# RetNet attention and maxout FFN on one core: blocks 6 and 7 worked in chunks

## The chip, the cores and the metric

One core of a Trainium2 chip runs the whole kernel. The metric is device time in microseconds of one execution. Besides the runs that give the time there is one profiled execution, from which all rows come.

## The reference

```python
# q, k, v: (8, 8, 576, 64) float32
scores = scale * q @ k.T
gamma = 1.0 - 2.0 ** (-5.0 - arange(8))                # one per head
Dmat = where(rel >= 0, gamma ** rel, 0.0)              # rel = row - column
attn = (scores * Dmat) @ v
x = attn.transpose(0, 2, 1, 3).reshape(4608, 512)
h = maximum(maximum(x @ w1, x @ w2), x @ w3)           # w: 512 x 768, float64 in memory
out = h @ w_out                                        # 768 x 512
```

The decay is a geometric one, so the kernel works in blocks of rows and carries a state (a sum of k times v) from block to block within a sequence.

## The kernel before, in words

The 4608 rows are cut into 36 blocks `g` of 128 rows. Four blocks make a tile `t` of 512 rows for the FFN; there are nine tiles. While `ffn(t)` runs the products of tile t, the list `steps(t + 1)` puts the attention steps of the next four blocks between them: the last loop of the kernel goes through twelve slots `at(0)` to `at(11)`, runs the steps of a slot, and then takes the next piece of `ffn(t)`. Each engine executes its instructions in the order in which they were recorded; semaphores hold an instruction until its inputs and its buffer are there. Nothing is scheduled at run time. Loads are issued on SP, the queue engine; a load that waits for its buffer holds all later loads.

For each block there are these steps:

- `load` brings k, q and v in rows (`kraw`, `qraw`, `vraw`). For blocks from `BY_PE` on, q is not brought in rows: `load_blocks` (L223) brings q and a second copy of k (`kxraw`) in squares of 32 by 32. Each of its DMAs moves 32 KB.
- `transposes` (L275): for blocks below `BY_PE`, TensorE transposes k and q in 128 by 128 tiles (L295, results `kt`, `qt`) and ScalarE copies them out (L296). From `BY_PE` on, VectorE does a StreamTranspose of 32 by 32 squares, one instruction for k and one for q, and the layout of the load does the rest.
- `decay` multiplies v by a factor; for blocks from `CPT + 2` = 6 on it is a list `scaling` of eight small ScalarE multiplies (L209), one for each head, that are put between other work, or all at once by `scores`.
- `scores`: the products k times q, and k times v for the state. Blocks 0 to 3 are in one form; below `BY_CHUNKS` is `parity_scores` (L322, L327, masks L338, states L346 and L348); from `BY_CHUNKS` on is `chunk_scores` (L377, L380; mask L384, states L392 on VectorE and a multiply L394 on GpSimd). Both use 64 matmuls of 64 by 64 for a pair of blocks away from the ends of a sequence.
- `values`: the products of the masked scores with v (L505 or L527), and of the old state with q (L496 or L534), for two blocks at once. `parity_values` makes the second in two halves, with two small ScalarE copies between them, which read what the first half wrote:

```python
        old(0)
        for m in range(2):
            nc.scalar.copy(first[:], o[m][:, 0, 0, 0:1])

        def rest():
            old(1)
            between.append(partial(chunk_output, o, chunks, t, i))

        between.append(rest)
```

- `chunk_output` then writes the result, scaled, into `xT`, the FFN's input; the last pair of a tile also starts the sums `xS`. What lies in `between` is recorded at the next place where `ffn` takes it.
- `carry` copies the parity form's state into the chunk form's state once, at the first block by chunks; `state_factors` copies the factors `gs_of`.

Tile 0 of the FFN is special. It is done in plain products: `up` (L930, nine units of two 128 x 512 results each), with maxima on VectorE (L935), then `down` (L917). In this time the weights arrive as float64 and are converted by ScalarE and VectorE (`convert`). A unit of the table `middles` has attention steps after its first result. From tile 1 on (first product at 119.04 us) the FFN is done in fewer products of sums (L905), which need the weight sums that VectorE makes at the end of tile 0. So blocks 4 to 7 are worked within tile 0, under `steps(1)`, with a, b, c, d = 4, 5, 6, 7.

Buffers that matter: q in rows or squares has two buffers `q` (blocks 2 and 5 have one of their own), `kx` has two, k three and one more; four PSUM banks `r` serve scores, values and, from block 4 on, TensorE's transposes.

Of the kernel before, what the change touches and what calls it, by code (L numbers as in the profile page):

```python
# [49 lines left out]
C = 128  # L50
NT = 4 * C
NH = NT // 2
BY_PE = 8
BY_CHUNKS = 8
AHEAD = 3
FILL = 160
PARTS = 11
# [42 lines left out]
def kernel(  # L100
# [14 lines left out]
    nc = tc.nc  # L115
    P = 128
# [3 lines left out]
    NP = H // 2  # L120
# [1 line left out]
    NDC = DM // P  # L122
    NF = DF // P
    CPT = NT // C
    assert B * S % C == 0 and S % D == 0 and BY_CHUNKS % CPT == 0 and S >= C and N % NT == 0 and NT % P == 0 and 2 * D == P and NP == NDC

    const = ctx.enter_context(tc.tile_pool(name="const", bufs=1))
    raw = ctx.enter_context(tc.tile_pool(name="raw", bufs=AHEAD + 1))
# [17 lines left out]
    def half(j):  # L146
        return slice(D * j, D * (j + 1))
# [59 lines left out]
    def scale(n=1):  # L207
        for _ in range(min(n, len(scaling))):
            scaling.popleft()()  # L209
# [33 lines left out]
                        src[b, :, pos:pos + 32, 32 * a:32 * a + 32].rearrange("h p i -> p h i"))  # L243

    def load(g, names="kqv"):
        if g >= BY_PE and ("q", g) not in raws:
            load_blocks(g, *range(C // 32))
        for n, src in (("k", k), ("q", q), ("v", v)) if g < BY_PE else (("k", k), ("v", v)):
            if n not in names:
                continue  # L250
            bufs = {"k": 3, "q": 2, "v": 4}[n]
            pool, bufs = (raw0, 1) if n != "v" and g < BY_PE and g % (bufs + 1) == bufs else (raw, bufs)
            if n == "v":
                t = vpool.tile([C, H, D], FP32, tag="v", name="vraw")
            else:
                t = pool.tile([C, H, D], FP32, tag=n, name=n + "raw", bufs=bufs)
            raws[n, g] = t
            for row, b, pos, m in spans(g):
                nc.sync.dma_start(t[row:row + m], src[b, :, pos:pos + m, :].rearrange("h p d -> p h d"))
# [147 lines left out]
        for j in range(2):  # L407
            nc.scalar.copy(stacked(g)[half(0), j::2, :], states[g][half(j)])

    def state_factors():  # L410
        for j in range(2):
            nc.scalar.copy(gs_of[half(0), j::2], gs[half(j)])

# [106 lines left out]
    def chunk_values(chunks, t, i):  # L520
        o = [ps_r.tile([P, 2, NP, D], FP32, tag="r", name="o") for _ in range(2)]
        cross = ((0, 0), (1, 1), (0, 1), (1, 0))
        for n, g in enumerate(chunks):
            for u in range(NP):
                for m, c in cross:
                    h = head(c, u)
                    nc.tensor.matmul(o[m][half(c), n, u, :], lhsT=vds[g][half(m), h, :], rhs=sts[g][half(m), h, :],  # L527
                                     start=n == 0 and u == 0, stop=place(g, m) == 0, skip_group_check=True)
        for n, g in enumerate(chunks):
            for u in range(NP):  # L530
                for m, c in cross:
                    h = head(c, u)
                    if place(g, m) > 0:
                        nc.tensor.matmul(o[m][half(c), n, u, :], lhsT=stacks[g][half(m), h, :],  # L534
                                         rhs=qks[g]["q"][half(m), h, :], start=False, stop=True, skip_group_check=True)
        chunk_output(o, chunks, t, i)

    def chunk_output(o, chunks, t, i):
        if i == 0:
# [420 lines left out]
    def ffn(t):  # L960

        h = hpool.tile([P, NF, NT], FP32, tag="h", name="h")
        if t == 0:
            a, b, c, d = range(CPT, 2 * CPT)
            middles = {units[2]: [(transposes, a)], units[3]: [(scores, a)], units[5]: [(scores, b)],
                       units[8]: [(scores, c, d)]}
            for fp, i in units:
                if (fp, i) == units[0]:
                    first_ups(h)
                    yield  # L970
                    continue
                for fb in (2 * fp, 2 * fp + 1):
                    maximum, = up_plain(t, h, fb, i)
                    if (fp, i) == units[-1] and fb % 2:
                        maximum()
                        convert(2)
                    else:
                        convert(4 if (fp, i) == units[1] else 2)
                        maximum()
                    for step, *blocks in middles.get((fp, i), ()) if fb == 2 * fp else ():  # L980
                        for g in blocks:
                            step(g)
                    scale(3)
                    if between:
                        between.pop()()
                yield
            convert(3)
            for fb, _ in enumerate(downs_plain(t, h, range(NF // 2))):
                convert(4 * len(pieces) if fb else 2)
                scale(4)  # L990
                if fb == 1:
                    while_converting.close()
                    late["pool"] = ctx.enter_context(tc.tile_pool(name="late", bufs=1))
                    state_factors()
                    nc.gpsimd.tensor_copy(causal[half(1), 0:D], causal[half(1), half(1)])
                    late_room()
                    weight_sums(0)
                if fb == 2:
                    between.pop()()
                chore((0, 2, 6, 6, len(chores), 0)[fb])  # L1000
                if fb == 3:
                    between.pop()()
                if fb in (1, 3):
                    yield
            yield
            return
        order = (0, 2, 1)
        if t == 1:
            spread.append(True)
            weight_sums(2)  # L1010
            weight_sums(1)
            form_groups = seven_forms(order)
        if t == 2:
            out_sums(order)
        total = len(order) * 2 * len(PRODUCTS)
        count = parts = 0
        for fp in order:
            while fp not in summed_fp:
                chore()
            for step, _ in enumerate(up(t, h, fp)):  # L1020
                if step % 4 == 1 or step % 4 == 3 and len(urgent) > (2 if t == 1 else 6):
                    chore(len(urgent) > 0)
                elif chores:
                    chores.popleft()()
                if step % 3 == 2:
                    scale()
                if t == 1 and fp == order[-1] and step == 19:
                    chores.extend(form_groups[0])
                count += 1
                if count * (NF // 2 * 3) >= (parts + 1) * total:  # L1030
                    parts += 1
                    yield
            if t == 1:
                seven_hidden(h, fp)
            elif fp != order[-1]:
                chores.extend(sums_of_hidden(h, order, 3 - order.index(fp)))
        chore(len(urgent) + len(chores))
        if t == 1:
            for n, _ in enumerate(downs_seven(t, order)):
                if n == 0:  # L1040
                    for step in form_groups[1]:
                        step()
                chore(4)
                scale(2)
                if n in (1, 3):
                    yield
        else:
            for n, _ in enumerate(downs(t, h, order)):
                chore(2)
                scale()  # L1050
                if n in (3, 9):
                    yield
        yield
# [52 lines left out]
    def steps(t):  # L1106
# [12 lines left out]
        if t == 1:  # L1119
            a, b, c, d = range(CPT, 2 * CPT)  # L1120
            at(0, (load, a, "kq"))
            at(1, (load, a, "v"))
            at(2, (load_weights, 2), (load, b, "kq"))
            at(3, (decay, a), (load, b, "v"), (load, c, "kq"))
            at(4, (transposes, b), (load, c, "v"))
            at(5, (decay, b), (load, d))
            at(6, (decay, c), (load_blocks, d + 1, 0))
            at(7, (values, [a, b]), (transposes, c), (finish_values, b), (decay, d), (convert, 2),
               (load_blocks, d + 1, 1, 2))
            at(8, (transposes, d), (load_blocks, d + 1, 3), (load, d + 1))  # L1130
            at(9, (load_blocks, d + 2, 0, 1))
            at(10, (values, [c, d]), (decay, d + 1), (load_blocks, d + 2, 2))
            at(11, (load_blocks, d + 2, 3), (load, d + 2), (transposes, d + 1))
            return todo
        for n in range(0, CPT, 2):
            a, b, m = CPT * t + n, CPT * t + n + 1, 6 * (n // 2)
            first_pair = a == BY_CHUNKS
            s = m + 2 if first_pair else m + 1
            at(m - (n > 0), (transposes, b))
            if first_pair:  # L1140
                at(m, (decay, b), (load, a + 2), (carry, a))
            at(s, (scores, a), (scores, b), (load, b + 2))
            at(s + 1, (decay, a + 2))
            at(s + 2, (decay, b + 2))
# [60 lines left out]
```

## Time and profile before

| | |
|---|---|
| median of 3 runs | 740.6 us (740.52 to 742.5) |
| profiled execution, its own time | 740.45 us |
| its span | 738.7 us |
| TensorE / VectorE / ScalarE / GpSimd busy | 733.8 / 568.8 / 356.6 / 36.4 us |
| granted TensorE clock | 1.0 |
| DMA | 58.85 MB, mean 80 GB/s; 222 to 261 GB/s in the first 74 us |

The span is what the trace sees from the first to the last instruction; the time has 1.75 us more around it. A row of the timeline gives start and length in us, engine, line, operation, output from input, sizes and the number of records; in brackets stands the idle time of the engine before it and what ended it. A matmul of float32 shows as two records. Lines of the kernel are written L295. A wait row gives who waited for whom: total, times, the longest.

### The profile page before, as it was taken

Reading aid. Unit: us, or ns where it says so; the run is one execution under the profiler, and the core shown is the slowest. Engines: PE = TensorE matmul, PEld = TensorE weight load, DVE = VectorE, ACT = ScalarE, POOL = GpSimd, SP = SyncE. Lnnn points to the kernel's source line nnn. Section 1 sums busy time; section 2 is a strip of 40 time slices with the busy share of each in tenths; the row PEclk is TensorE's granted clock in tenths of the full one; section 3 lists DMA queues with packets and bytes.
Section 4 is the critical chain, followed back from the end, with each engine's and each line's share of the span. In section 5 each row is a group of like instructions: output and inputs, shape, how many; then the busy total and the mean of one; then the engine's idle time right before and its main releaser. Section 6 shows DMA issues by size and latency. Waiting matters only on the chain.

```text
span 738.7 us, 17318 instructions
## 1 busy us (share of the span) xinstructions
PE 733.8 (99%) x6948; PEld 606.1 (82%) x6948; DVE 568.8 (77%) x1051; ACT 356.6 (48%) x746; POOL 36.4 (5%) x42
## 2 busy tenths in 40 slices
PE   9999999999999999999999999999999999999998
PEld 7654546888888888888888888888888888888887
DVE  5998697999886895699658876787768966893676
ACT  4896934554245534544354525543455255424441
POOL 2000000122000100010000000000100010000000
PEclk9999999999999999999999999999999999999999
DMA  9999523414251515141524243332514150000001
GB/s 222 243 246 261 120 54 85 87 24 93 68 97 29 96 37 104 40 87 39 109 50 75 48 107 60 60 58 58 115 23 94 42 121 14 1 31 29 0 1 57
DMA packets 226640, 58.85 MB, mean 80 GB/s; under 512 B 207872, under 2 KB 225280, under 8 KB 226560
## 3 DMA queue, kind: packets, MB, share of 16 engines
q1 hardware_dynamic: 225584, 57.71, 36.0%
q8 instruction: 54, 0.88, 0.5%
q14 instruction: 26, 0.21, 0.1%
q10 hardware_dynamic: 976, 0.04, 0.1%
HBM read 48.27 MB, written 9.44 MB: 78 GB/s over the span
## 4 chain that ended last, share of the span: by engine, by line
PE 99%; DVE 0%; ACT 0%; issue 0%
PE a L905 20%; PE b L905 17%; PE c L905 9%; PE up L930 9%; PE di L751 7%; PE d L905 6%; PE e L905 6%; PE dhc L751 5%; PE deg L751 3%; PE sk L377 3%; PE down L917 3%; PE o L527 2%; PE dfd L751 2%; PE o L534 2%; PE dx L658 1%; PE kv L380 1%
## 5 line engine op out<-in xcount | busy, mean ns | idle before, releaser
L893 DVE TENSOR_TENSOR part<-part 128x512 f32<-128x512 f32 x168 | 117.8, 701 | 86.4 <-ACT part L890 83.8
L890 ACT COPY part<-b 128x512 f32<-128x512 f32 x120 | 70.3, 586 | 163.6 <-PE b L905 161.0
L893 DVE TENSOR_TENSOR h<-h,part 128x512 f32<-128x512 f32 x120 | 83.2, 693 | 24.9 <-ACT h L890 20.5
L890 ACT COPY part<-a 128x512 f32<-128x512 f32 x96 | 56.3, 586 | 51.6 <-PE a L905 51.1
L209 ACT ACTIVATE vraw<-vraw,gk 128x64 f32<-128x64 f32 x240 | 76.8, 347 | 0.1
L905 PE MATMUL b<-s,n 128*128 128x256 f32 x288 | 73.9, 379 | 0.0
L930 PE MATMUL up<-xT,w 128*128 128x512 f32 (+2 forms) x160 | 64.0, 554 | 0.0
L905 PEld LDWEIGHTS b<-s,n 128*128 128x128 f32 x288 | 54.7, 190 | 7.4
L930 PEld LDWEIGHTS up<-xT,w 128*128 128x128 f32 x160 | 28.4, 190 | 29.2 <-issue 26.1
L740 ACT COPY k<-di 128x256 f32<-128x256 f32 x49 | 18.2, 372 | 68.5 <-PE di L751 42.1
L905 PE MATMUL c<-xT,w 128*128 128x256 f32 x192 | 51.2, 389 | 0.0
L394 POOL TENSOR_TENSOR s<-s,gs_of 64x512 f32<-64x512 f32 x21 | 22.5, 1070 | 558.2 <-DVE s L392 441.8
L905 PE MATMUL d<-s,w 128*128 128x256 f32 x192 | 49.8, 380 | 0.0
L905 PE MATMUL b<-xT,n 128*128 128x256 f32 x192 | 49.3, 379 | 0.0
L905 PE MATMUL a<-xT,w 128*128 128x256 f32 x192 | 49.3, 379 | 0.0
L905 PE MATMUL a<-s,w 128*128 128x256 f32 x192 | 49.3, 379 | 0.0
L905 PE MATMUL e<-xT,w 128*128 128x256 f32 x192 | 45.4, 379 | 0.0
L905 PE MATMUL a<-xT,n 128*128 128x256 f32 x192 | 45.4, 379 | 0.0
L905 PEld LDWEIGHTS e<-xT,w 128*128 128x128 f32 x192 | 36.5, 190 | 5.4 <-issue 0.5
L905 PEld LDWEIGHTS a<-s,w 128*128 128x128 f32 x192 | 36.5, 190 | 5.0
L905 PEld LDWEIGHTS a<-xT,w 128*128 128x128 f32 x192 | 36.5, 190 | 5.0
L905 PEld LDWEIGHTS b<-xT,n 128*128 128x128 f32 x192 | 36.5, 190 | 5.0
(200 smaller groups left out, 1386.4 us busy)
## 6 DMA issues: line engine op xcount, KB each, us to landing
bits<-in_moe_w_dram SPq DMA_DIRECT2D x36, 256.0 KB, 5.7
kraw<-in_k_dram SPq DMA_DIRECT2D x32, 256.0 KB, 3.1
vraw<-in_v_dram SPq DMA_DIRECT2D x32, 256.0 KB, 3.6
qraw<-in_q_dram SPq DMA_DIRECT2D x224, 32.0 KB, 2.1
kxraw<-in_k_dram SPq DMA_DIRECT2D x224, 32.0 KB, 2.1
out_dram<-osb SPq DMA_DIRECT2D x56, 128.0 KB, 1.7
bits<-in_moe_w_out_dram SPq DMA_DIRECT2D x6, 512.0 KB, 5.1
qraw<-in_q_dram SPq DMA_DIRECT2D x7, 256.0 KB, 5.4
```

What stands on the lines that cost most here:

```text
L209: scaling.popleft()()
L377: nc.tensor.matmul(s[half(c), h, :], lhsT=kT[half(c), h, :], rhs=qT[half(c), h, :], start=True, stop=True)
L394: nc.gpsimd.tensor_tensor(new, new, factor, op=ALU.mult)
L527: nc.tensor.matmul(o[m][half(c), n, u, :], lhsT=vds[g][half(m), h, :], rhs=sts[g][half(m), h, :], start=n == 0 and u == 0, stop=place(g, m ...
L534: nc.tensor.matmul(o[m][half(c), n, u, :], lhsT=stacks[g][half(m), h, :], rhs=qks[g]["q"][half(m), h, :], start=False, stop=True, skip_gro ...
L740: nc.scalar.copy(place, a)
L751: nc.tensor.matmul(banks[chain], lhsT=hidden(h, order, b, late_ones)[:, e], rhs=late["V"][v][:, e], start=begins and e == 0, stop=chain no ...
L890: nc.scalar.copy(of[step], ps[step[0]][:])
L893: nc.vector.tensor_tensor(of[dst], a, b, op=op)
L905: nc.tensor.matmul(ps[chain][:, e, :], lhsT=factor(w, 2 * fp + e), rhs=xS[t][x], start=n == 1 and e == 0, stop=ends, skip_group_check=True)
L917: nc.tensor.matmul(b[:], lhsT=h[:, fb, m * P:(m + 1) * P], rhs=w_sb["out", fb], start=fb == blocks[0], stop=fb == blocks[-1])
L930: nc.tensor.matmul(ps[:, a:b], lhsT=w_sb[i, fb][:, dc * P:(dc + 1) * P], rhs=xT[t][:, dc, a:b], start=dc == 0 and a == 0, stop=dc == NDC - ...
```

## The change

`BY_PE` and `BY_CHUNKS` go from 8 to 6: blocks 6 and 7 are loaded in 32 by 32 squares, transposed by VectorE, and worked by `chunk_scores` and `chunk_values`. Their square loads are recorded at slots 6 and 7, behind k and v and all weights but the last two pieces. Block 6's VectorE transposes and `carry` stand at slot 8, block 7's in the middle of the last unit of `up`, and the scores of both behind that unit. The loads of blocks 8 and 9 move from slots 6 to 11 to slots 9 to 11. The values of blocks 6 and 7 are no longer split, their outputs go through `between`, and the factors and the second half of the mask are made earlier by `chunk_constants`.

```diff
-BY_PE = 8
-BY_CHUNKS = 8
+BY_PE = 6
+BY_CHUNKS = 6
...
     def load(g, names="kqv"):
-        if g >= BY_PE and ("q", g) not in raws:
+        if g >= BY_PE and "q" in names and ("q", g) not in raws:
             load_blocks(g, *range(C // 32))
...
-    def state_factors():
+    def chunk_constants():
+        nc.gpsimd.tensor_copy(causal[half(1), 0:D], causal[half(1), half(1)])
         for j in range(2):
             nc.scalar.copy(gs_of[half(0), j::2], gs[half(j)])
...   # end of chunk_values
-        chunk_output(o, chunks, t, i)
+        if spread:
+            chunk_output(o, chunks, t, i)
+        else:
+            between.append(partial(chunk_output, o, chunks, t, i))
...   # ffn, t == 0
-            middles = {units[2]: [(transposes, a)], units[3]: [(scores, a)], units[5]: [(scores, b)],
-                       units[8]: [(scores, c, d)]}
+            middles = {units[2]: [(transposes, a)], units[3]: [(scores, a)], units[5]: [(scores, b), (chunk_constants,)],
+                       units[8]: [(transposes, d)]}
...
                     scale(3)
+                    if (fp, i) == units[8] and fb % 2:
+                        scores(c)
+                        scores(d)
                     if between:
                         between.pop()()
...   # ffn, t == 0, the down products
-                    state_factors()
-                    nc.gpsimd.tensor_copy(causal[half(1), 0:D], causal[half(1), half(1)])
                     late_room()
                     weight_sums(0)
-                if fb == 2:
+                if between:
                     between.pop()()
                 chore((0, 2, 6, 6, len(chores), 0)[fb])
-                if fb == 3:
-                    between.pop()()
...   # steps(1)
-            at(3, (decay, a), (load, b, "v"), (load, c, "kq"))
+            at(3, (decay, a), (load, b, "v"), (load, c, "k"))
             at(4, (transposes, b), (load, c, "v"))
-            at(5, (decay, b), (load, d))
-            at(6, (decay, c), (load_blocks, d + 1, 0))
-            at(7, (values, [a, b]), (transposes, c), (finish_values, b), (decay, d), (convert, 2),
-               (load_blocks, d + 1, 1, 2))
-            at(8, (transposes, d), (load_blocks, d + 1, 3), (load, d + 1))
-            at(9, (load_blocks, d + 2, 0, 1))
-            at(10, (values, [c, d]), (decay, d + 1), (load_blocks, d + 2, 2))
-            at(11, (load_blocks, d + 2, 3), (load, d + 2), (transposes, d + 1))
+            at(5, (decay, b), (load, d, "kv"))
+            at(6, (decay, c), (load_blocks, c, 0, 1, 2, 3))
+            at(7, (values, [a, b]), (finish_values, b), (decay, d), (convert, 2), (load_blocks, d, 0, 1, 2, 3))
+            at(8, (transposes, c), (carry, c))
+            at(9, (load, d + 1))
+            at(10, (values, [c, d]), (load_blocks, d + 2, 0, 1))
+            at(11, (decay, d + 1), (load_blocks, d + 2, 2, 3), (load, d + 2), (transposes, d + 1))
             return todo
...   # steps(2) and on
-            first_pair = a == BY_CHUNKS
+            first_pair = t == 2 and n == 0
...
-                at(m, (decay, b), (load, a + 2), (carry, a))
+                at(m, (decay, b), (load, a + 2))
```

## The prediction

> **What bounds the kernel now.** I read the page's busy times first, then the chain that ended last, then TensorE's own timeline around the blocks that the change touches.
>
> ```profile
> span 738.7 us, 17318 instructions
> PE 733.8 (99%) x6948; PEld 606.1 (82%) x6948; DVE 568.8 (77%) x1051; ACT 356.6 (48%) x746; POOL 36.4 (5%) x42
> PE 99%; DVE 0%; ACT 0%; issue 0%
> ```
>
> TensorE is busy for 733.8 of 738.7 us and the chain is TensorE from end to end. The missing 4.9 us are no holes in the middle, as the table of windows shows (span; then busy time and count of TensorE, its weight loads, VectorE, ScalarE, GpSimd; clock, DMA share, GB/s):
>
> ```profile
> 0.00:20.00 20.00, 18.19 (x228) 15.22 (x230) 11.18 (x29) 8.96 (x15) 5.30 (x14) 1.00 1.00 227
> 20.00:730.00 710.00, 710.00 (x6699) 586.25 (x6696) 553.84 (x1016) 346.54 (x729) 31.15 (x28) 1.00 0.35 75
> ```
>
> Of 710 us TensorE is idle in none, at a granted clock of 1.00. So a gain can only be TensorE work that goes away, and a loss must be a new hole in TensorE. The timeline of TensorE from 75 us on shows both blocks (score lines between 90.30 and 92.32 are left out):
>
> ```profile
> 75.74 1.16 PE L505 MATMUL o<-m,vd 64*64 64x64 f32 x64
> 76.72 0.64 PE L496 MATMUL o<-qT,state 64*64 64x64 f32 x24
> 77.29 0.66 PE L295 MATMUL kt<-ident,kraw 128*128 128x128 f32 x4
> 77.78 0.60 PE L295 MATMUL qt<-ident,qraw 128*128 128x128 f32 x4
> 78.31 0.68 PE L496 MATMUL o<-qT,state 64*64 64x64 f32 x24
> 78.93 7.13 PE L930 MATMUL up<-xT,w 128*128 128x512 f32 x16
> 85.90 0.60 PE L295 MATMUL kt<-ident,kraw 128*128 128x128 f32 x4
> 86.33 0.60 PE L295 MATMUL qt<-ident,qraw 128*128 128x128 f32 x4
> 86.77 3.60 PE L930 MATMUL up<-xT,w 128*128 128x512 f32 x8
> ...
> 92.32 3.70 PE L930 MATMUL up<-xT,w 128*128 128x512 f32 x8
> 95.86 7.03 PE L917 MATMUL down<-w_out,h 128*128 128x512 f32 x16
> 102.82 1.16 PE L505 MATMUL o<-m,vraw 64*64 64x64 f32 x64
> ```
>
> Columns are start, length, and the count of records (two per matmul). A stage is worth the step from its start to the next start, because lengths overlap. Read so, the L295 transposes of block 6 hold TensorE for 78.31 - 77.29 = 1.02 us and those of block 7 for 86.77 - 85.90 = 0.87 us.
>
> **What goes from TensorE.** Blocks 6 and 7 are now transposed on VectorE: 1.02 + 0.87 = 1.89 us less.
>
> Their scores stay 64 matmuls for the pair. Before, they took 92.32 - 90.30 = 2.02 us; the pairs by chunks take 2.02 to 2.09 us (243.03 to 245.05 and 164.15 to 166.24). I count 0 and keep 0.07 for the range. Their values were split by a `down` group: 104.38 - 102.82 = 1.56 plus 108.64 - 108.01 = 0.62, so 2.18 us. In one piece, as chunks are, a pair takes 184.93 - 182.84 = 2.09 in one place and 261.95 - 259.93 = 2.02 in another; I take 2.02, so 0.16 less, at the least 0.09.
>
> **What merges.** Each visit to another kind of matmul costs a restart. `up` in groups of 8, 16 and 24 records takes 3.53, 6.97 and 10.40 us: 3.43 for each further 8. Between the values of blocks 4, 5 and the scores of 6, 7 there are now 32 records in a row, 10.40 + 3.43 = 13.83, instead of 6.97 + 3.53 + 3.54 = 14.04: 0.21 less. Likewise the last 32 `down` records: 13.83 instead of 3.63 + 10.40 = 14.03: 0.20 less. If the restarts are only an effect of modelled ends, these two terms are nothing.
>
> **What opens: the cover of a ScalarE copy.** In `parity_values` the second half `old(1)` waits for two tiny `first` copies on ScalarE, which wait for the end of `old(0)`. For blocks 4 and 5 the transposes of block 6 stood between, and hid this:
>
> ```profile
> 76.33 0.82 ACT L209 ACTIVATE vraw<-vraw,gk 128x64 f32<-128x64 f32 x3
> 77.42 0.35 ACT L509 COPY first<-o 128x1 f32<-128x1 f32 x2 [0.27 <-PE o L496]
> 77.98 0.59 ACT L296 COPY kT<-kt 128x512 f32<-128x512 f32 x1 [0.22 <-PE kt L295]
> ```
>
> ScalarE is free 0.27 us before the first copy, and its order up to it is the same afterwards. The copies end at 77.42 + 0.35 = 77.77; TensorE then starts some 0.05 us later (the scores at 19.69 start 0.05 after the copy they wait for). So `old(1)` starts at 77.82, where the next work started at 77.29: 0.53 us of hole. For blocks 6 and 7 the copies disappear, and there is no hole. Bounds: 0 if the wait ends under the drain that TensorE has anyway, 0.82 (a group of three L209 multiplies) if ScalarE comes late.
>
> **What VectorE and GpSimd get.** Four StreamTransposes of 0.67 to 0.70 us, 2.8 us; masks and states stay about the same (before, per block, 0.76 + 0.87 + 0.42 = 2.05 us; by chunks 3 x 0.69 = 2.07). VectorE is idle for 4.8 of the 24 us from 78 to 102 (19.22 busy), so they fit. A new link is GpSimd's multiply L394 (1.03 to 1.48 us) between block 6's state and block 7's. I followed it: the scores of 6 and 7 end at 78.43 (restart of `up`) + 13.83 + 2.02 = 94.3. VectorE first does a maximum (0.69) and two conversion steps (1.22 + 1.22) from 92.3 on, then mask and two adds (2.07), to 97.5; GpSimd ends at about 98.7, or 99.1 by its slow case; block 7's adds end by 100.5. The values of 6 and 7 start at 94.3 + 6.96 (16 `down` records) = 101.3, and need block 7's state only in their second half at 102.3. 1.8 us remain: cost 0, at worst some 1 us if VectorE runs late. ScalarE's two `carry` copies (0.82 together) move ahead of block 7's scores; it loses four L296 copies (2.3 us) in the same stretch. The first sums of the next products need VectorE's conversion and weight sums to end by about 118, which its 2.8 extra us still allow.
>
> **What the queue on SP gets.** Removed are the two 256 KB loads of q; added are 32 loads of 32 KB, and blocks 8 and 9 (32 of the same) move behind. In front of block 8, SP used to wait for block 6's transposes:
>
> ```profile
> SPq L241 <- PE qt L295: 8.6, 1, 8.6
> 78.42 0.83 SPq L241 DMA_DIRECT2D qraw<-in_q_dram  x2
> 79.29 0.93 SPq L241 DMA_DIRECT2D kxraw<-in_k_dram  x2
> 80.33 0.87 SPq L601 DMA_DIRECT2D bits<-in_moe_w_out_dram  x2
> 99.98 0.45 SPq L259 DMA_DIRECT2D kraw<-in_k_dram  x1
> ```
>
> Block 6 needs no such wait: its buffers were block 3's, free since about 18 us. It stands behind the second pair of `w_out` pieces, issued at 68.41 and landed near 74.4; with 512 KB less ahead of it at the 248 GB/s of the stretch 16 to 70, 2 us sooner, near 72.4. From there issues are the pace: 0.49 us apart, with stalls; block 8's sixteen plus two `w_out` pieces took from 78.42 to 88.27 to issue and block 9's from 89.45 to 99.98, so 10 us a block, and 2.2 us from issue to landing. About eight loads were open at a time, so half of block 6 can be issued by 72.4; the other 8 plus two `w_out` pieces plus 16 of block 7 go out by about 87, and land by 89. VectorE comes to block 7's transposes at 90.8 and TensorE needs them at 93.3. Block 6 is needed at 87 and lands by 80. Block 8 then waits for block 6's VectorE transposes (88), block 9 for block 7's, and they end by 110; VectorE wanted block 8's at 114.65. What queues behind SP's wait is the output of the first tile, 117 us. Cost 0; the price beyond the slack is the second rival.
>
> The Trainium skill, "DMA: Bandwidth & Descriptors", section "Specifications", speaks against this change: pieces under 512 B do not reach line rate, and these are of 128 B. The trace shows the stretch 78 to 102, with such loads, at 116 GB/s against 248 with long pieces. If only transfer at 116 GB/s counted, the 1 MB of both blocks would take 9 us, the pace above 16 to 20; neither reaches TensorE's need.
>
> **The sum.** 1.89 + 0.16 + 0.21 + 0.20 - 0.53 = 1.93 us less. The profiled execution took 740.45 us around its span of 738.7, and the median of the three runs is 740.6. So 740.45 - 1.93 = 738.5.
>
> About 0.3%, 2.2 us, is what a measurement of this kernel can tell from no change: 738.4 from the median. The forecast lies almost on that line, just inside.
>
> **The rivals.** (1) The wait for the `first` copies costs nothing: 1.89 + 0.16 + 0.21 + 0.20 = 2.46 less, 738.0. For it: TensorE's ends are modelled, and a drain may already be in the 0.62 us of `old(1)`. Against: the two copies are real and last in line. (2) Block 7's loads come late. TensorE needs both transposes (1.4 us) done by 93.3, so from a landing after 92.0 on each us costs one; at 93.9 the gain is gone. If block 7 could only be issued when block 6 has landed, at the paces of blocks 8 and 9 (11.4 and 12.2 us to the last landing) from 72.4 on, it lands at 96.0: 4.0 us of hole, 740.45 - 1.93 + 4.0 = 742.5; with another hiccup of 1 to 2 us, as SP shows at 85 and 97, over 743. Against: no buffer couples the two blocks. (3) The chain over GpSimd ends late and VectorE costs 1 us: 739.5. (4) The transposes leave TensorE but the restarts gain nothing: 1.89 + 0.16 - 0.53 = 1.52 less, 738.9; this is the forecast's own upper end.
>
> **How the numbers follow.** The forecast, with 738.1 to 738.9, has 0.55, of which 0.2 below 738.4. Rival 1 has 0.17, rival 3 0.13, rival 2 0.15, of which 0.1 over 742.8. So faster 0.2 + 0.17 = 0.37, slower 0.1, same 0.53. The range reaches from 737.6 (rival 1 with nothing lost at all) to 741.0, into the light cases of rival 2; what it leaves out is some 0.05 below and 0.13 above.
>
> **What would show it.** Right: L295 with a quarter fewer records (blocks 0 to 5 instead of 0 to 7), TensorE about 2 us less busy, a hole of about 0.5 us on TensorE near 77.3 ended by the `first` copies, SP no longer waiting 8.6 us for `qt`, first L905 near 117.1 where it was 119.04, and nothing changed after. Wrong: a hole at 92 to 94 ended by VectorE's transposes or by a DMA of `kxraw`, one at 101 to 103 ended by GpSimd's L394, a hole near 77 that is missing or twice as long, or any gain after 119.

## The result, and the profile after

The changed kernel takes 738.85 us in the median of nine runs (738.46 to 739.42) against 740.49 us for the kernel before on the same chip; the ratio is 0.9975, with a 95% interval of 0.9964 to 0.9985. That is a gain of 1.64 us between the medians and 1.85 by the ratio; the interval reaches from 1.1 to 2.7 us. The interval of the ratio does not reach 1, so there is a gain, though it is smaller than the 0.3% that the prediction set as its line. The profiled execution took 738.46 us around a span of 736.7. Two executions of kernels below, of 1279.67 and 1523.25 us, were disturbed and are in no ratio.

From the page of the changed kernel, span and busy times:

```profile
span 736.7 us, 17316 instructions
PE 731.4 (99%) x6932; PEld 604.1 (82%) x6932; DVE 572.3 (78%) x1051; ACT 354.6 (48%) x740; POOL 39.1 (5%) x44
```

TensorE has 16 records less and 2.4 us less to do; VectorE has 3.5 us more. TensorE's timeline from 75 us on (score lines left out; an L number above 500 or 900 is the line of before plus one or four):

```profile
75.64 1.16 PE L506 MATMUL o<-m,vd 64*64 64x64 f32 x64
76.62 0.64 PE L497 MATMUL o<-qT,state 64*64 64x64 f32 x24
77.53 0.68 PE L497 MATMUL o<-qT,state 64*64 64x64 f32 x24 [0.27 <-ACT first L510]
78.14 14.00 PE L934 MATMUL up<-xT,w 128*128 128x512 f32 x32
...
94.11 7.13 PE L921 MATMUL down<-w_out,h 128*128 128x512 f32 x16
101.18 1.16 PE L528 MATMUL o<-m,vraw 64*64 64x64 f32 x64
102.16 1.11 PE L535 MATMUL o<-qT,s 64*64 64x64 f32 x64
103.20 14.00 PE L921 MATMUL down<-w_out,h 128*128 128x512 f32 x32
117.04 1.89 PE L909 MATMUL e<-xT,w 128*128 128x256 f32 x8
```

The reader sees the four L295 lines gone, one `up` of 32 records where three stood, the values of blocks 6 and 7 in one piece, and one bracket: TensorE idle for 0.27 us until ScalarE's `first` copy. From the values of blocks 4 and 5 to the first L909 product it is 117.04 - 75.64 = 41.40 us, where it was 119.04 - 75.74 = 43.30. Step by step, each from its start to the next start:

| step | before | after | difference | predicted |
|---|---|---|---|---|
| transposes of blocks 6, 7 | 1.89 | 0 | -1.89 | -1.89 |
| values of blocks 4, 5 | 2.17 | 2.50 | +0.33 | +0.53 |
| `up`, 32 records | 14.04 | 13.93 | -0.11 | -0.21 |
| scores of blocks 6, 7 | 2.02 | 2.04 | +0.02 | 0 |
| `down`, first 16 records | 6.96 | 7.07 | +0.11 | 0 |
| values of blocks 6, 7 | 2.19 | 2.02 | -0.17 | -0.16 |
| `down`, last 32 records | 14.03 | 13.84 | -0.19 | -0.20 |
| sum | 43.30 | 41.40 | -1.90 | -1.93 |

The steps are worked out from the printed starts, so one can differ by 0.01 from the prediction's. They run from a start to a start, so that modelled ends do not enter them. The second half of the values of blocks 4 and 5 starts 0.91 us after the first (77.53 - 76.62), where TensorE went on after 0.57 (77.29 - 76.72): the hole is 0.34 us, and the half itself is 0.01 shorter. From the first L909 on, the two traces run alike: 616.6 and 616.5 us to the end of the last matmul.

VectorE's and GpSimd's part of the chain that could have become the bound:

```profile
86.67 0.70 DVE L221 STREAM_TRANSPOSE kT<-kxraw 128x512 f32<-128x512 f32 x1
90.39 0.70 DVE L221 STREAM_TRANSPOSE kT<-kxraw 128x512 f32<-128x512 f32 x1
91.02 0.67 DVE L221 STREAM_TRANSPOSE qT<-qraw 128x512 f32<-128x512 f32 x1
97.34 0.69 DVE L384 TENSOR_TENSOR m<-sk,causal 128x512 f32<-128x512 f32 x1
98.55 1.41 DVE L392 TENSOR_TENSOR s<-kv,s 64x512 f32<-64x512 f32 x2 [0.52 <-POOL s L394]
```

Block 7's transposes end at 91.69 and TensorE comes for them at 93.1. GpSimd's multiply, 97.48 to 98.52, makes VectorE wait 0.52 us, and block 7's state is there at 99.96, over 2 us before TensorE reads it.

At L241 SP waited 8.6 us for `qt` before; the longest wait that it has there now is:

```profile
SPq L241 <- DVE qT L221: 2.3, 1, 2.3
```

Block 6's squares land from 70.9 to 76.7 us, block 7's from 81.9 to 87.36. VectorE does not wait for either.

### The profile page after: what moved, and what is told of

Its sections match the earlier page's. It is cut to its first block, busy times and chain, and to the rows that moved or that the text cites. A ratio compares the mean times of both kernels' runs of the same rounds, so it can differ in the third digit from the quotient of the medians.

```text
span 736.7 us, 17316 instructions
## 1 busy us (share of the span) xinstructions
PE 731.4 (99%) x6932; PEld 604.1 (82%) x6932; DVE 572.3 (78%) x1051; ACT 354.6 (48%) x740; POOL 39.1 (5%) x44
## 4 chain that ended last, share of the span: by engine, by line
PE 97%; SPq 1%; DMA 1%; issue 0%; ACT 0%; DVE 0%
PE a L909 20%; PE b L909 17%; PE c L909 9%; PE up L934 9%; PE di L755 7%; PE d L909 6%; PE e L909 6%; PE dhc L755 5%; PE deg L755 3%; PE sk L377 3%; PE down L921 3%; PE o L528 2%; PE o L535 2%; PE dfd L755 2%; PE dx L662 1%; SPq L259 1%
## 5 line engine op out<-in xcount | busy, mean ns | idle before, releaser
L909 PE MATMUL b<-s,n 128*128 128x256 f32 x288 | 73.9, 379 | 0.0
L909 PEld LDWEIGHTS b<-s,n 128*128 128x128 f32 x288 | 54.7, 190 | 7.4
L394 POOL TENSOR_TENSOR s<-s,gs_of 64x512 f32<-64x512 f32 x23 | 25.0, 1089 | 553.6 <-DVE s L392 476.5
L909 PE MATMUL c<-xT,w 128*128 128x256 f32 x192 | 51.3, 389 | 0.0
L909 PE MATMUL d<-s,w 128*128 128x256 f32 x192 | 49.8, 380 | 0.0
L909 PE MATMUL b<-xT,n 128*128 128x256 f32 x192 | 49.3, 379 | 0.0
L909 PE MATMUL a<-s,w 128*128 128x256 f32 x192 | 49.3, 379 | 0.0
L909 PE MATMUL a<-xT,w 128*128 128x256 f32 x192 | 49.3, 379 | 0.0
L909 PE MATMUL e<-xT,w 128*128 128x256 f32 x192 | 45.4, 379 | 0.0
L909 PE MATMUL a<-xT,n 128*128 128x256 f32 x192 | 45.4, 379 | 0.0
L909 PEld LDWEIGHTS e<-xT,w 128*128 128x128 f32 x192 | 36.5, 190 | 5.4 <-issue 0.5
L909 PEld LDWEIGHTS b<-xT,n 128*128 128x128 f32 x192 | 36.5, 190 | 5.0
L909 PEld LDWEIGHTS a<-s,w 128*128 128x128 f32 x192 | 36.5, 190 | 5.0
L909 PEld LDWEIGHTS a<-xT,w 128*128 128x128 f32 x192 | 36.5, 190 | 5.0
```

What stands on the lines that cost most here:

```text
L394: nc.gpsimd.tensor_tensor(new, new, factor, op=ALU.mult)
L909: nc.tensor.matmul(ps[chain][:, e, :], lhsT=factor(w, 2 * fp + e), rhs=xS[t][x], start=n == 1 and e == 0, stop=ends, skip_group_check=True)
```

## The experiments

Ratios are against the kernel before, run beside each kernel; the changed kernel's is 0.9975. Differences in us to the changed kernel are between medians that were not taken beside each other; by the ratios they come out up to 0.25 us smaller or 0.1 larger.

**The transposes back on TensorE.** A step that writes 8 transposes of k which nobody reads, at the two old places.

```diff
+    def spare_transposes(g):
+        for _ in range(2):
+            pt = ps_r.tile([P, NP, C], FP32, tag="r", name="kt")
+            for p in range(NP):
+                nc.tensor.transpose(pt[:, p, :], pair(raws["k", g], p), ident[:C, :C])
...
-            at(7, (values, [a, b]), (finish_values, b), ...
+            at(7, (values, [a, b]), (spare_transposes, c), (finish_values, b), ...
-            at(8, (transposes, c), (carry, c))
+            at(8, (transposes, c), (spare_transposes, d), (carry, c))
```

> The changed kernel with 16 transposes of 128 by 128 put back on TensorE where they stood before: 8 of block 6's k between the two halves of the values of blocks 4 and 5, and 8 of block 7's k behind the next unit; their results are not read. The loads, VectorE's transposes and the chunk form stay. Our theory (the gain is TensorE's work): 1.02 + 0.87 us come back, the hole of 0.27 us is covered again, `up` is cut once more for 0.1: 1.65 us more than the changed kernel, 740.5, as before the change. Rival (the gain is the queue's or comes from the chunk form): 738.9.

Measured: 740.48 us, ratio 0.9994 (0.9985 to 1.0003). The kernel cannot be told from the one before, and is 1.63 us above the changed kernel (1.4 by the ratios) for an expected 1.65. Its timeline shows the old pattern, with no bracket:

```profile
77.16 1.09 PE L522 MATMUL kt<-ident,kraw 128*128 128x128 f32 x8
78.18 0.68 PE L497 MATMUL o<-qT,state 64*64 64x64 f32 x24
78.79 7.13 PE L940 MATMUL up<-xT,w 128*128 128x512 f32 x16
85.76 1.04 PE L522 MATMUL kt<-ident,kraw 128*128 128x128 f32 x8
86.64 7.03 PE L940 MATMUL up<-xT,w 128*128 128x512 f32 x16
```

From the values of blocks 4 and 5 to the first product it is 118.57 - 75.60 = 42.97 us: 1.57 of the 1.90 us are gone. All that the change does to loads, VectorE and GpSimd is still in this kernel. So most of the gain is TensorE's 16 transposes, less the hole that they covered, and not the queue's. The other 0.33 us, still saved here, are in the pieces that the change merges: 0.17 in the values of blocks 6 and 7, the rest in `up` and `down`.

**The queue alone.** The kernel before, where block 6's q goes into the buffer of blocks 2 and 5.

```diff
-            pool, bufs = (raw0, 1) if n != "v" and g < BY_PE and g % (bufs + 1) == bufs else (raw, bufs)
+            pool, bufs = (raw0, 1) if n != "v" and g < BY_PE and (g % (bufs + 1) == bufs or n == "q" and g == 6) else (raw, bufs)
```

> The kernel before, but block 6's q takes the separate buffer of blocks 2 and 5, so block 8's squares no longer wait for block 6's transposes: SP's wait of 8.6 us goes, and blocks 8 and 9 land some 6 to 8 us sooner. TensorE's work is untouched. Our theory: 740.5, no change, and no hole less. Rival (the freed queue is what gains): 738.6 to 739.

Measured: 740.82 us, ratio 1.0002 (0.9993 to 1.0011). Block 8's squares begin at 67.13 us where they began at 78.42, and nothing gets faster. SP then waits 6.3 us for block 7's transposes instead.

**No transposes in the kernel before.** ScalarE copies blocks 6 and 7 untransposed.

```diff
             src = raws["k", g] if n == "k" else raws.pop(("q", g))
+            if g >= CPT + 2:
+                nc.scalar.copy(both[n][:], src[:].rearrange("a (p two) d -> a p (two d)", two=2))
+                continue
```

> The kernel before, but blocks 6 and 7 are not transposed: ScalarE copies k and q as they lie into the tiles for the transposed ones, so the scores of these blocks are of untransposed data, and nothing else changes: the loads, SP's wait and the parity form stay. Our theory (the gain is TensorE's work): 1.89 us of transposes go, a hole of 0.35 to 0.5 us opens at the `first` copies of blocks 4 and 5, `up` merges for 0.1: 1.5 to 1.65 us less than the kernel before, 738.9 us. Rival (the gain is the queue's, whose 8.6 us wait the change removes): 740.5, no change.

Measured: 740.0 us, ratio 0.9992 (0.9983 to 1.0001): only half of what we expected, and not to be told from no change by the time. From the values of blocks 4 and 5 to the first product it is 42.42 us, 0.88 less than before. The 1.89 us are gone and the hole costs 0.34; the rest is a wait that we had left out. TensorE comes to the scores at 89.84, and ScalarE makes the last four factors of v at this time:

```profile
90.01 1.15 ACT L787 ACTIVATE expo<-expo,inf 128x1024 int32<-128x1024 int32 x1
91.07 1.05 ACT L209 ACTIVATE vraw<-vraw,gk 128x64 f32<-128x64 f32 x4
```

TensorE waits for these multiplies: from 91.25 us on its matmuls start in groups (at 91.25, 91.69, 91.85, 92.17 and 92.33), and the scores take 2.70 us, 0.68 more than before. The saved time has turned into a new wait. The changed kernel puts the scores behind the last `up` group, and the next experiment shows what that is worth.

**The scores at their old place.**

```diff
-                       units[8]: [(transposes, d)]}
+                       units[8]: [(transposes, d), (scores, c, d)]}
...
-                    if (fp, i) == units[8] and fb % 2:
-                        scores(c)
-                        scores(d)
```

> The changed kernel with the scores of blocks 6 and 7 back where they were before, between the two results of the last unit of `up`, 3.4 us sooner. Our theory (TensorE must not come to block 7's scores before VectorE's transposes, which end at 91.69 us, and before ScalarE's multiplies of v): the scores start at 88.55, block 7's would start at 89.6 and wait until 91.8: a hole of 2.2 us, and 0.1 for the extra cut: 741.1 us, the gain is gone; more if the clock falls after the hole. Rival (the place of the scores does not matter, the gain is the missing transposes alone): 738.9.

Measured: 741.72 us, ratio 1.0015 (1.0006 to 1.0024): slower than the kernel before. Its rows come from a further execution:

> The changed kernel with the scores of blocks 6 and 7 back between the two results of the last unit of `up`, once more for its profile, which was taken in a disturbed execution. Measured before: 741.72. Our theory: a hole of about 2.2 us inside the scores ended by VectorE's transpose, and up to 0.6 us of half clock or of waiting for ScalarE. Rival: the loss is elsewhere, in `down` or in the first L909 products.

That execution took 741.17 us. The hole lies where it was expected:

```profile
92.24 0.33 PE L377 MATMUL sk<-qT,kT 64*64 64x64 f32 x4 [2.03 <-DVE qT L221]
```

From values to first product it is 43.76 us, 2.36 more than the changed kernel's 41.40, for an expected 2.3. Without the moved scores, the moved transposes lose.

**Block 7's squares later, by 8 and by 16 loads.** More loads of squares of k, into a tile that nobody reads, in front of block 7's.

```diff
+    def load_twice(g, rounds):
+        t = raw0.tile([P, H, D // 32, 32], FP32, tag="spare", name="spare", bufs=1)
+        for m in range(8 * rounds):
+            ...   # one square load, as in load_blocks
...
-            at(7, ..., (convert, 2), (load_blocks, d, 0, 1, 2, 3))
+            at(7, ..., (convert, 2), (load_twice, d, rounds), (load_blocks, d, 0, 1, 2, 3))
```

> The changed kernel with 8 more 32 KB loads (squares of k into a spare tile that nothing reads) ahead of block 7's squares: its last square lands near 91.3 us, VectorE's transposes end at 92.7, TensorE needs them at 93.1. Our theory (slack first, then one for one): no hole, 738.9 us; VectorE stands still for some 0.9 us. Rival (no slack, each us of landing costs): 4 us more, 742.8.

> The changed kernel with 16 more 32 KB loads (squares of k into a spare tile that nothing reads) just ahead of block 7's squares. At 0.49 us each, block 7's last square lands near 95.3 in place of 87.36 us, VectorE's two transposes end near 96.7, and TensorE needs them at 93.1 (second half of the scores). Our theory (from a landing of 91.7 on, each us costs one): a hole of about 3.6 us on TensorE inside the scores, ended by VectorE's transpose; 742.4 us, slower than the kernel before. Rival (the slack is larger, or the queue takes the extra loads faster): under 1 us, 738.9 to 739.8. Rival (the late queue also hits the tile after): over 5 us.

With 8 loads: 740.83 us, ratio 1.0001 (0.9988 to 1.0015), and the runs scatter from 738.85 to 744.26. We expected no hole; in the profile there is one of 1.22 us. The last square landed at 93.47, and not at 91.3: SP needed 5.87 us for the eight, and began them at 78.24, where it began block 7's squares at 76.01 in the changed kernel. From the landing the two transposes and the hand-over take 1.58 us, and TensorE starts at 95.05. Its scores take 3.59 us in place of 2.04, so 1.55 more.

```profile
DVE kT L221 <- DMA kxraw<-in_k_dram: 2.5, 1, 2.5
PE sk L387 <- DVE qT L221: 1.2, 1, 1.2
```

With 16: 748.74 us, ratio 1.0106 (1.0092 to 1.0120), 9.9 us more than the changed kernel for an expected 3.6. The loads came later than we had reckoned here too: the last square landed at 99.67 in place of 95.3 (SP began the sixteen at 79.77 and needed 8.99 us), and the hole is 7.42 us. And there is a second price, which neither theory had. Windows of this kernel (start, end, length, then busy time and count of TensorE, its weight loads, VectorE, ScalarE, GpSimd; granted clock, DMA share, GB/s):

```profile
92.66:103.27 10.61, 3.19 (x129) 2.96 (x128) 3.44 (x5) 2.02 (x2) 0.00 (x0) 0.68 0.39 61
103.27:112.04 8.77, 8.77 (x18) 3.60 (x17) 7.98 (x10) 1.06 (x4) 2.52 (x2) 0.80 0.61 114
112.04:127.90 15.86, 15.86 (x161) 8.14 (x161) 15.72 (x40) 1.76 (x3) 0.00 (x0) 1.00 0.32 71
```

The granted clock is 0.5 from 96.49, inside the hole, until 106.73: the 16 records of `down` take 8.77 us where they take 7.07. Of 51.67 - 41.40 = 10.27 us more, 7.42 are the hole, and 1.70 are the slower `down`; most of the rest is the second half of the scores, which takes 2.03 us from its first matmul to `down` where it took 1.00.

**The squares at their old slots.**

```diff
-            at(3, ..., (load, c, "k"))
+            at(3, ..., (load, c, "kq"))
-            at(5, (decay, b), (load, d, "kv"))
-            at(6, (decay, c), (load_blocks, c, 0, 1, 2, 3))
-            at(7, ..., (convert, 2), (load_blocks, d, 0, 1, 2, 3))
+            at(5, (decay, b), (load, d))
+            at(6, (decay, c))
+            at(7, ..., (convert, 2))
```

> The changed kernel with the squares of blocks 6 and 7 at the slots where their q was loaded before (3 and 5), ahead of v, of part of the up weights and of w_out. Our theory: 16 issues of 0.49 us and 512 KB of short pieces for each block stand in a stretch where the DMA engines are full, so the weights behind them land 3 to 8 us later for each block; ScalarE and VectorE convert late, and `up` or `down` waits: 1 to 8 us more than the changed kernel, 740 to 747. Rival (the place of the squares does not matter, since the conversion has that much slack): 738.9.

Measured: 744.48 us, ratio 1.0049 (1.0032 to 1.0067), 5.6 us over the changed kernel. The last pieces of the `up` weights land at 71.55 in place of 61.76 us, the second pair of `w_out` pieces at 90.40 in place of 70.72. `up` does not wait, against our guess; ScalarE and VectorE do, and through them the scores:

```profile
ACT expo L778 <- DMA bits<-in_moe_w_dram: 6.8, 1, 6.8
ACT expo L778 <- DMA bits<-in_moe_w_out_dram: 4.2, 1, 4.2
PE kv L380 <- ACT vraw L209: 2.0, 1, 2.0
PE sk L377 <- DVE qT L221: 1.6, 1, 1.6
```

The two waits of TensorE are 3.66 us of the 6.46 that the trace has more from values to first product; 1.69 are `down` again, 8.76 us for 7.07, at a granted clock of 0.5 from 100.39 to 103.80. So the place of the squares, behind most weights, is a condition of the gain.

**Blocks 4 and 5 as well.** `BY_PE` and `BY_CHUNKS` are 4, `carry` and `chunk_constants` stand before block 4, the values of blocks 4 and 5 are not split, and their factored v has a tile of another pool.

> The changed kernel taken further: blocks 4 and 5 too are loaded in squares and worked by chunks, with their loads at the slots of their q. Our theory: TensorE loses two more pairs of transposes (0.87 + 0.87 us), the hole of 0.34 us and some restarts, 2.2 us in all: 736.6, if the weights stay in time; but 32 more issues stand in the first 60 us, where the DMA engines are full, so weights land 3 to 8 us later for each block. If the conversion has no slack this costs more than it brings: 738 to 747. Likeliest: slower than the changed kernel. Rival (slack is enough): 736.6.

Measured: 753.22 us, ratio 1.0166 (1.0150 to 1.0182). TensorE waits 7.02 us, until 51.70, for a converted weight and 4.90 us, until 105.91, for block 7's transposes. ScalarE's conversion waits 14.6 us for loads of weights between 20 and 130 us. So the further loads made the weights late, as our theory had it.

**The hole covered.** The second half of the values of blocks 4 and 5 one `up` group later.

```diff
-            at(7, (values, [a, b]), (finish_values, b), (decay, d), ...
+            at(7, (values, [a, b]), (decay, d), ...
```

> The changed kernel, with the second half of the values of blocks 4 and 5 recorded one `up` group later, so that a group of `up` covers the two `first` copies. Our theory (the hole is real, each visit to another kind of matmul costs a restart): the hole of 0.34 us between 77.19 and 77.53 goes, but the values are split (2.18 in place of 2.02 us) and the 32 `up` records are cut (about 0.1 us); the values and `up` together get shorter by 0.1 to 0.2 us, 738.7 us, not to be told from the changed kernel. Rival (restarts are only an effect of modelled ends): 0.4 us less, 738.4. Rival (the copies cost more than the trace shows): over 1 us less.

Measured: 738.98 us, ratio 0.9976 (0.9965 to 0.9986): no change that can be told. In the trace the hole is gone; the values take 1.55 + 0.62 = 2.17 us in place of 2.50, and `up` in two pieces 3.63 + 10.50 = 14.13 in place of 13.93. From values to first product it is 41.26 us, 0.14 less, as expected. The times cannot refute the rival's 0.4 us less.

**The price of a cut, many times.** The values of 13 later pairs are cut in two, the second half recorded one slot later.

> The changed kernel, with the values of the 13 pairs of blocks from 10 on cut into their two halves, the second a slot later, between other products. Same matmuls. Our theory (each visit to another kind of matmul costs a restart): each cut costs 0.16 us of values and about 0.05 of the products around, 13 x 0.21 = 2.7 us more: 741.6. Rival (restarts are only modelled in the trace): 738.9, and the two terms of 0.16 and 0.2 in the prediction were no gain. More than 5 us would be another wait, to be looked for in the trace.

Measured: 764.94 us, ratio 1.0333 (1.0315 to 1.0350). As a measurement of time this failed: the later second halves delay the sums on VectorE, and TensorE waits for them in most tiles (at 369.3 us for 2.96 us, ended by VectorE's `osb`). Where nothing waits, the trace shows the cut: values in two pieces of 1.09 us where 2.02 stood, and 80 records of L905's products in 5.81 + 11.85 = 17.66 where they take 17.46, so 0.36 us a cut, from start to start. The run's own time shows nothing of it, because of the waits.

**The scatter at the start.** Block 3's k is loaded ahead of the first weight pieces.

```diff
     load(2, "kq")
+    load(CPT - 1, "k")
     load_weights(1)
     load(2, "v")
-    load(CPT - 1, "kq")
+    load(CPT - 1, "q")
     load_weights(1)
```

> The changed kernel with block 3's k loaded ahead of the first two weight pieces. In every trace TensorE waits for this load at 16 to 17 us, 0.17 to 1.27 us, and that is where executions of one kernel differ. Our theory (the start decides the rest of the scatter): the wait goes and the weights' first conversion, which has 1.5 us of slack, takes the delay: 0.3 to 0.6 us less than the changed kernel, 738.4, faster than both. Rival (the weights become late): up to 1 us more, 739.9.

Measured: 739.84 us, ratio 0.9987 (0.9978 to 0.9996): 1.0 us above the changed kernel (0.9 by the ratios, whose intervals overlap), so our theory, which had it faster, fell. The wait for k is gone, but block 2's v now lands later:

```profile
POOL vd L270 <- DMA vraw<-in_v_dram: 5.8, 1, 5.8
PE kv L423 <- POOL vd L270: 0.8, 1, 0.8
```

The loss is not the weights', as the rival had it: the first conversion waits 2.2 us, but `up` does not. Whether v is the cause stays open: from the values of blocks 4 and 5 to the first product it is 41.40 us as in the changed kernel, and these values start at 76.47, 0.83 later, which kernels with an unchanged start do as well (next section). Nor is the wait for k in every trace: TensorE has none in the kernels with 8 more loads and with the transposes put back. We found no version that beats the changed kernel by more than a run can tell.

## Why the prediction was right

- **What bounds it:** TensorE, end to end. A gain had to be TensorE's work, and it was: putting 16 transposes back took 1.57 of the 1.90 us away in the trace, and freeing the queue alone gave nothing.
- **The sum:** 1.93 us less predicted; 1.90 in the trace between the values of blocks 4 and 5 and the first product, 1.64 between the medians. That it came out within 0.03 us is in part luck: the hole cost 0.20 less than written and the merged pieces gave 0.21 less. The times alone, at 1.1 to 2.7 us, could not tell the forecast from rivals 1 and 4. The two traces of the pair start these values 0.10 us apart. Over all profiled executions, TensorE comes there between 75.56 and 76.84 us in kernels that are the same up to there (left out are the kernel that fills the first 60 us with more loads and the execution of 1279.67 us). Most of the later ones have a longer wait for block 3's k (0.17 us in the kernel before, 1.00 in the latest), but one comes at 76.23 without it. This scatter is larger than what remains of the difference.
- **The hole at `first`** was predicted at 0.53 and measured at 0.34. The step that was mis-sized: we let `old(1)` wait for both copies. Its first matmuls write the tile whose copy comes first (block 4 has products into this tile alone), and TensorE started at 77.53, between the copies' ends at 77.48 and 77.67.
- **The restarts** were counted wrongly. The values of blocks 6 and 7 gave 0.17, near the 0.16 predicted. For `up` and `down` the prediction counted pieces and wrote 0.41; the rows show 0.1 us for each border with 64 by 64 matmuls. Each further 8 records take 3.43 us; 8 alone take 3.53 with one such border (86.77 before) and 3.63 with two (104.38). The 128 by 128 transposes beside them cost nothing of this kind: with the transposes back, `up` in two pieces takes 6.97 + 6.96 = 13.93 us, as in one. Before, `up` and `down` had seven borders and now they have five: the scores that left the middle of `up` stand in front of `down`. So 0.11 and 0.19 were gained and 0.11 lost again in the first 16 records of `down`, 0.2 in all.
- **Rival 4**, by which the restarts gain nothing, gave 738.9 us, and the median of 738.85 is nearer to it than to the forecast of 738.5. Only the trace speaks against it: 1.90 us from start to start for its 1.52. Of these 0.38, 0.2 are a smaller hole, and 0.2 the merged pieces.
- **Rival 1** (the hole costs nothing) fell by the bracket in the trace and by the starts, 0.34 us apart.
- **Rival 2** (block 7 late) is real, with the point where it starts (a landing near 91.5 to 92.1) as predicted (TensorE's need at 93.11 less 1.58 for transposes and hand-over is 91.53), and a landing at 87.36 where 89 was reckoned: some 4 us of slack. Its price was set too low: with 8 more loads a landing 1.4 us beyond the point cost 1.55, about what was said, but with 16 the longer hole also cost clock.
- **Rival 3:** GpSimd's multiply ended at 98.52 (98.7 predicted), and TensorE did not wait.
- **Some figures of the prediction** rest on less than it says. The 184.93 in its values of 2.09 us is the end of a row; the next start is 184.86, so the step is 2.02 there too, and the 0.07 kept for the range is no spread of the values. Its lower bound of 737.6 is not worked out; rival 1's own sum gives 738.0. And the 116 GB/s from 78 to 102 us was not shown to be a limit of short pieces: the DMA engines were busy for 0.55 of that stretch, against 1.04 from 16 to 70.
- **What was left out:** ScalarE's multiplies of v. The prediction followed VectorE and the squares to the scores, and named ScalarE only in passing; with the scores at their old place that would have been a wait of its own, as the kernel without transposes shows. In the changed kernel the last one ends at 91.9, some 1.2 us before TensorE comes to block 7's scores.

## What to carry to other kernels

When one engine is busy all the time, count the work that leaves it, step by step from start to next start, and then look at what that work had covered: a copy's latency here, and two other engines' lead at the scores. A saving on the bound is kept only if nothing behind it then waits; with the transposes gone and the scores at their old place, 0.88 us were saved in the trace, because 0.68 came back as a wait for ScalarE. Where matmuls of two kinds alternate, count the borders between them and not the pieces: here each border with 64 by 64 matmuls cost 0.1 us. Before work is given to a queue, look at what is queued behind it: the same loads cost 5.6 us when they stood ahead of the weights.

## What the runs showed of the hardware that we had not expected

A hole in TensorE's work can cost more than its length. After the hole of 7.42 us the granted clock was 0.5 until 5.5 us after its end. After holes of 1.61 and 2.05 us within 6 us, in the kernel with the squares at their old slots, it fell too, while one hole of 2.03 us alone, in the profile of the early scores, left it at 1.00. With the values cut, it fell after 1.47 and 0.54 us within 3.2 us:

```profile
284.96 1.13 PE L917 MATMUL b<-s,n 128*128 128x256 f32 x4 [1.47 <-DVE osb L586]
286.63 1.76 PE L917 MATMUL a<-xT,w 128*128 128x256 f32 x4 [0.54 <-DVE k L586]
288.19 1.91 PE L917 MATMUL c<-s,w 128*128 128x256 f32 x4
```

The four records that take 1.03 us take 1.76 and 1.91, and the granted clock from 287 to 291 was 0.57. But almost the same two holes stand in this trace twice more, from 449.74 and from 530.99 us on, and there the clock stayed at 1.00. The second time:

```profile
532.45 1.13 PE L917 MATMUL b<-s,n 128*128 128x256 f32 x4 [1.46 <-DVE osb L586]
534.12 1.13 PE L917 MATMUL a<-xT,w 128*128 128x256 f32 x4 [0.54 <-DVE k L586]
```

The trace shows what differs. The granted clock changes at 208.48, 211.89, 286.99, 290.40, 368.91 and 372.32 us, and the times between these are whole multiples of 3.41 us (75.10 is 22 of them, 78.51 is 23). So it changes on a grid that does not start anew with a hole. Windows on this grid, the later two counted on from 372.32 (after the length of the window comes TensorE's busy time; its granted clock is the third number from the end):

```profile
283.58:286.99 3.41, 1.49 (x6) 1.01 (x7) 2.48 (x8) 0.58 (x1) 0.00 (x0) 1.00 0.57 199
286.99:290.40 3.41, 3.41 (x10) 2.69 (x9) 2.19 (x5) 0.80 (x2) 0.00 (x0) 0.50 0.31 101
529.32:532.73 3.41, 1.95 (x9) 1.42 (x8) 0.77 (x3) 0.00 (x0) 0.00 (x0) 1.00 0.93 263
532.73:536.15 3.42, 2.88 (x13) 2.20 (x13) 3.39 (x9) 1.17 (x2) 0.00 (x0) 1.00 0.41 143
```

The first pair of holes lay in one window and left 1.49 of its 3.41 us busy; the pair from 530.99 on lay in two. In the kernel with the squares at their old slots, whose clock changes at 100.39 and 103.80, a window with 1.79 us busy (93.56 to 96.98) lowered nothing, and the next, with 1.36, did. So in these two traces a window with 1.92 us or more idle halved the clock for the next, and one with 1.63 us or less did not.

The Trainium skill, "TensorE: Matmul & The Clock Gate", section "What's actually happening", tells of a clock gate that goes back to half speed after an idle window of about 3.4 us. The length agrees with the grid, but by these runs a window need not be idle in full.
